# Last pass of a two-layer attention and feed-forward kernel with its gradients: wq read once in full rows, all four groups' products taken in the last head group

## The chip, the cores and the metric

The kernel runs on one core of one Trainium2 chip. The core has TensorE (PE: matmuls and transposes, which write PSUM), VectorE (DVE), ScalarE (ACT), GpSimd (POOL) and SyncE (SP), an on-chip memory SBUF, and 16 DMA engines that move data between SBUF and the chip's main memory. SP issues all loads here and POOL all stores, so there are two DMA queues: SP's (q1 in the profile) and POOL's (q0). Each engine works through its own instruction stream in order.

The metric is the device time of one execution in microseconds. Before the change, the median of three runs is 1944.12 us (1943.76, 1944.12 and 1950.13). About half a per cent, 9.7 us, is what a measurement of this kernel can tell from no change.

## The reference

The forward function is applied to one token `x` (1 x 1024), against a key and a value cache, with the same weights used twice:

```python
def _A_ref(x, k_cache, v_cache, wq, wo):          # 32 query heads, 4 kv heads, 65536 keys, 128 per head
    q = (x @ wq).reshape(B, Sq, Hq, Dh).transpose(0, 2, 1, 3)
    ...
    scores = jnp.einsum("bhqd,bhkd->bhqk", q, k) * (Dh ** -0.5)
    o = jnp.einsum("bhqk,bhkd->bhqd", softmax(scores), v)
    return o.transpose(0, 2, 1, 3).reshape(B, Sq, Hq * Dh) @ wo
def _B_ref(x, w1, b1, w2, b2):                    # 1024 -> 3584 -> 1024, squared relu
    ...
x = x + _A_ref(_layernorm(x), k_cache, v_cache, wq, wo)
x = x + _B_ref(_layernorm(x), w1, b1, w2, b2)
x = x + _A_ref(_layernorm(x), k_cache, v_cache, wq, wo)
x = x + _B_ref(_layernorm(x), w1, b1, w2, b2)
```

The result is that `x` (out_0) and, for a given `grad_out`, the gradients to the input (out_1), the key cache (out_2), the value cache (out_3), wq (out_4), wo (out_5), w1 (out_6), b1 (out_7), w2 (out_8) and b2 (out_9). All inputs and outputs are bfloat16. Each cache is 4 x 65536 x 128, that is 67 MB, and so is its gradient.

## The kernel before, in words

**Four passes over the caches.** The two forward attentions are passes 0 and 1. The backward of the second attention is pass 2, which needs only the gradient to its queries. Pass 3, the last, computes the query gradient of the first attention and the gradients of both caches (which take parts from both attentions), and stores everything that is large. Between the passes stand dense stages for the feed-forward layers. The names in the code are `attn_fwd`, `attn_bwd3` and `attn_bwd4`; the kernel's PSUM flag `PS["pass4"]` is set in the last pass, which begins near 1185 us.

**Items and steps.** A pass goes over four head groups (one per kv head, eight query heads each), and over the 512 columns of 128 keys of each group in items of eight. `pipeline` (L840) runs one step per item: in each step it calls every stage on the item that is due at that stage's lag, and then `bg.step`, which runs one piece of background work. The last pass has 256 items, 64 per group. Its first stage (values, `vT`) leads the others by up to 16 steps and its last (`k8`, L1445, which folds keys into the query gradient) trails by 11 (`B4_LAG`). After the last item of a group `k8` calls `on_group(g)`, here `on4`: from then on the query gradient `dqT` of that group is known.

**Blocks of 1 MB.** SBUF holds an arena of 20 blocks of 1 MB (128 partitions of 8 KB). `Slot` takes a block, `free` gives it back. Eight of the blocks hold the softmax numerators of both attentions, two per group; they come free as the groups of the last pass end. In the last pass blocks are kept in two classes: a ring for blocks that will be stored (`fill=True`), which starts with two blocks, grows to five (`NRING`) and gets two more at the end of each group, and the rest for loads. A load can start when its block's last reader is done.

**Who sets the order.** In passes 0 to 2 the engines' streams keep the order of the program (`manual_schedule`). In the last pass they don't: a planner simulates the program with its own idea of each instruction's duration and, on each engine, puts next the earliest instruction of the program that it takes to be ready. An instruction late in the program can so be moved ahead of others. What the planner expects of a load need not be what the chip does, and on the chip the streams are fixed.

**Background work of the last pass.** `Background.step` (L786) first serves `urgent` generators, one piece per step; a generator that yields `"wait"` lets the `normal` ones have the step. Urgent are:

- `g_dO` (L965), the gradient to the first attention's output for the next group, through `g_rowdots` (L577) over eight slabs of wo;
- `g_dn` (L992), added by `on4` for each of the first three groups: the share of this group's `dqT` in the gradient `dn1` to the layer norm's output, also through `g_rowdots`, over eight slabs of wq.

`g_rowdots` multiplies a slab (128 rows of the weight, 1024 columns) by a vector that `g_bcast_vec` (L559) has spread over all partitions, on VectorE (L598), and sums each row on ScalarE (L587):

```python
        steps = 8 if PS["pass4"] else WAIT_STEPS
        ...
            t = mvs.tile([P, n], BF, name="mv_t", tag="mv_t", bufs=2)
            nc.vector.tensor_tensor(out=t[:, :], in0=slab, in1=vbc[:, :], op=ALU.mult)
```

Slabs come four to a load of 1 MB: for wo, 8 KB that lie together per partition (`wo_runs`, L495); for wq, four pieces of 2 KB per partition, since a group's 1024 columns are a quarter of a row (`wq_slabs`, L487). The second load of a generator is issued when the first block has been used up, and `steps` waits are put ahead of its first product.

Normal are the outer products for the weight gradients (`g_outer`, `g_outer_wide`, `gwq`: two-row matmuls, L1504, whose results go to an arena block through `evac` and from there to memory) and `g_biases`.

**The last group.** Its `dqT` is known only at the very end, so its share is worked out by another way. `pre_load("wq4", ...)` loads its eight slabs in two loads 20 steps before the end, into two blocks. `fill4`, 10 steps before the end, takes two more blocks (`Rows`, L612), turns the slabs on TensorE (`front`, L661, 64 transposes at L682) and copies them, then drains the background. When `on4` is called for the last group, `PRE["rows"].run()` multiplies the turned slabs by `dqT` on TensorE (`back`, L707), and the layer norm's backward, out_1 and the last quarter of out_4 (`g_outer_last`, L1507, stores at L1525) follow.

**Copies out of PSUM.** `evac` (L150) gives each copy to ScalarE or VectorE by a running account of both loads. In `outer16` (L1418) it makes the results of the cache gradients, two copies of 128 x 1024 per step, and every second step a block is stored (L1432).

**The forward output.** `side_x4` (L1849) accumulates the last feed-forward product beside the dense stage between passes 2 and 3, adds it up after that stage's w2 slabs, and calls `col_to_dram` (L202) at once: a transpose on TensorE, a copy on VectorE, a store by POOL.

Of the kernel before, what the change touches and what calls it, by code (L numbers as in the profile page):

```python
# [3 lines left out]

# [12 lines left out]
P = 128  # L17
# [3 lines left out]
def kernel(  # L21
# [128 lines left out]
    def evac(out, in_, kind="bf"):  # L150
# [11 lines left out]
        else:  # L162
            load["dve"] += cd
            nc.vector.tensor_copy(out=out, in_=in_)  # L164


    def col_from_dram(v1d, n, name):
        nj = n // P
# [387 lines left out]
        return t  # L556


    def g_bcast_vec(vcol, nj):  # L559
# [5 lines left out]
        vbc = mvs.tile([P, nj * P], BF, name="vbc", tag="vbc", bufs=1)  # L565
        yield
        for j0 in range(0, nj, 4):
            pg = ps_gg() if PS["pass4"] else ps_tr([P, 512], F32)
            for jj in range(4):
                nc.tensor.matmul(pg[:, jj * P:(jj + 1) * P], lhsT=ident_b[0:nj, j0 + jj:j0 + jj + 1].to_broadcast([nj, P]),  # L570
                                 rhs=rows[0:nj, :], start=True, stop=True)
            nc.scalar.copy(out=vbc[:, j0 * P:(j0 + 4) * P], in_=pg[:, 0:512])
            add_load(act=0.6)
            yield
        return vbc

    def g_rowdots(slab_it, nk, vcol, nj, finish, name):  # L577
        n = nj * P
        y = vec.tile([P, nk], F32, name=name)
        nc.gpsimd.memset(y[:], 0.0)  # L580
        vbc = None
        due = None
        steps = 8 if PS["pass4"] else WAIT_STEPS

        def total(t, kc):
            def f():
                nc.scalar.activation(out=t[:, :], in_=t[:, :], func=ACTF.Copy, accum_out=y[:, kc:kc + 1])  # L587
            return f
        for kc, slab in slab_it:
# [8 lines left out]
            nc.vector.tensor_tensor(out=t[:, :], in0=slab, in1=vbc[:, :], op=ALU.mult)  # L598
# [12 lines left out]

    class Rows:  # L612
        def __init__(self, pool=None, bufs=NWT):
            self.pool, self.bufs = pool, bufs
            self.views = deque()
            self.n = 0
            self.parts = 0
            if pool is None:

                for _ in range(2):  # L620
                    t = Slot("s_wt").t[:, :].rearrange("p (v a b) -> p v a b", v=4, a=8)
# [667 lines left out]
    def attn_bwd4(p, La, Lb, on_group, bg, stack, end=()):  # L1289
# [128 lines left out]
        def outer16(name, out, key, xt, gg, j1):  # L1418

            if j1 == 0:  # L1420
                state[key] = Slot(name, True)
            stg = state[key].t[:, :].rearrange("p (j d) -> p j d", d=DH)
            for m in range(2):
                pg = ps_gg()
                for h in range(2):
                    nc.tensor.matmul(pg[:, 512 * h:512 * h + 512], lhsT=xt[64 * h:64 * h + 64, j1 // 8 + m, :],  # L1426
                                     rhs=gg[64 * h:64 * h + 64, :, :].rearrange("p a b -> p (a b)"),
                                     start=True, stop=True, tile_position=(64 * h, 0))
                jj = j1 + 8 * m
                evac(stg[:, jj:jj + 8, :].rearrange("p j d -> p (j d)"), pg[:, :], kind="f32")  # L1430
            if j1 + 16 == J:
                nc.gpsimd.dma_start(out=out, in_=stg)  # L1432
                state.pop(key).free(stored=True)
# [415 lines left out]
    def side_x4(kc, slab):  # L1849
        for nb in range(DC):  # L1850
            nc.tensor.matmul(ps_x4[:, nb, :], lhsT=d_cols(slab, nb), rhs=L4["gb"][:, kc:kc + 1].to_broadcast([P, 64]),
                             start=kc == 0 and nb == 0, stop=kc == FC - 1 and nb == DC - 1, skip_group_check=True)
        add_load(pe=DC * 0.03)
        if kc == FC - 1:
            f = tmp.tile([P, DC], F32, name="ffn_f")
            nc.vector.tensor_tensor(out=f[:], in0=ps_x4[:, :, 0], in1=b2c[:], op=ALU.add)
            nc.vector.tensor_tensor(out=x4[:], in0=x3[:], in1=f[:], op=ALU.add)
            col_to_dram(x4, D, out_0.rearrange("a b d -> (a b d)"))
    rows.add(w2_slabs()[0], FC, DC, lambda: dx2[:], fin_dh2, mix=True, side=side_x4)
    rows.add(w1_slabs()[0], DC, FC, lambda: dh2[:], fin_dx1, cols=f_cols, mix=True)  # L1860
    rows.add(wo_slabs(firstg[3])[0], R, DC, lambda: dx1[:], dO_finish(L1, firstg[3]), inplace=True)
# [15 lines left out]
    bg.total = 2 + n_outer(FC, DC) + n_outer(DC, FC, True) + n_outer(HQ, DC) + (G - 1) * n_outer(DC, DC)  # L1877
    bg.steps = len(ITEMS[3]) - 4
    dn1 = vec.tile([P, DC], F32, name="dn1")

    def g_biases():
        gb2 = tmp.tile([P, DC], F32, name="gb2")
        nc.vector.tensor_tensor(out=gb2[:], in0=gx[:], in1=dx2[:], op=ALU.add)
        col_to_dram(gb2, D, out_9)
        yield
        gb1 = tmp.tile([P, FC], F32, name="gb1")
        nc.vector.tensor_tensor(out=gb1[:], in0=dh4[:], in1=dh2[:], op=ALU.add)
        col_to_dram_f(gb1, F, out_7)
        yield
# [3 lines left out]
    def gwq(g):  # L1893
        return g_outer(bgpool, out_4, DC, R, [L3["n"], L1["n"]], [L3["dqT"][:, gsl(g)], L1["dqT"][:, gsl(g)]], c0=g * 1024)

    def on4(g):
        if g != lastg[3]:
            bg.add(g_dn(L1, dn1, g, g == firstg[3]))
            bg.normal.append(gwq(g))
        else:  # L1900
            next(PRE["gwq"])
            PRE["rows"].run()
# [22 lines left out]
    ps4_stack.close()  # L1925

# [29 lines left out]
```

## Time and profile before

| What | Value |
|---|---|
| Median of three runs | 1944.12 us |
| The profiled execution's own time | 1939.92 us |
| Its span, from the first to the last instruction | 1938.1 us |
| Moved by DMA in the span | 787.63 MB, 406 GB/s on average |
| Busy share of the span: PE, DVE, ACT, POOL | 82%, 60%, 54%, 7% |
| SP's queue (loads), share of the 16 DMA engines' time | 77.2% |
| POOL's queue (stores) | 20.5% |
| Busy in 1757 to 1922 us (165 us): PE, DVE, ACT | 138.0, 120.3, 116.1 us |

"L598 DVE" is an instruction of line 598 on VectorE. In a table of stretches, each row gives the stretch, its length, the busy time of PE, PE's weight loads, DVE, ACT and POOL with the number of instructions, then TensorE's granted clock as a share of full speed, the mean busy share of the 16 DMA engines (it can read 1.01 where packets overlap a little), and the GB/s that they moved. In a timeline a row gives the start, the duration, the engine, the line, the operation and what it writes and reads; a bracket at the end gives how long the engine sat idle before it and what ended that; "issue" there is a wait that the profile puts down to nothing.

### The profile page before, as it was taken

The page shows a single profiled execution, that of the slowest core. Times are in us where ns is not written, and L with a number is a line of the kernel's source. Part 1 is how long each engine was busy: PE and PEld are TensorE (multiplying, and loading weights), DVE is VectorE, ACT ScalarE, POOL GpSimd, SP SyncE. Part 2 cuts the span into 40 slices and gives each one's busy share as a digit, 9 for nine tenths or more (in the row PEclk, how much of TensorE's full clock was granted, in tenths as well). Part 3 has the DMA queues.
Part 4 walks back from the last instruction along what each step waited for, and adds up shares of the span by engine and source line. Part 5 has one row for each costly group of instructions (what it writes and reads, how often), then busy time and mean ns, then how long its engine had stood idle before and what let it go on. Part 6 is the DMA issues. An engine that isn't in the chain of part 4 may idle for free. (4 is left out here: it accounts for less than half of the span.)

```text
span 1938.1 us, 66986 instructions
## 1 busy us (share of the span) xinstructions
PE 1585.2 (82%) x30199; PEld 1301.4 (67%) x30199; DVE 1170.3 (60%) x2453; ACT 1044.9 (54%) x1617; POOL 142.2 (7%) x321
## 2 busy tenths in 40 slices
PE   6878778688777888977787898889997987697987
PEld 6878777678777877877776886555554654454554
DVE  5655555255555554545454567777775886685876
ACT  3444334245433545445363455766875885575775
POOL 0000000000000000000000001121111211121211
PEclk9999899689999999998899999898997998797998
DMA  9999999999999998999999988999999999899998
GB/s 393 427 425 425 429 427 415 391 407 423 427 425 429 428 422 309 377 425 429 426 424 421 408 314 308 425 424 389 425 424 413 419 424 424 345 419 397 424 422 352
DMA packets 107149, 787.63 MB, mean 406 GB/s; under 512 B 9440, under 2 KB 16622, under 8 KB 42222
## 3 DMA queue, kind: packets, MB, share of 16 engines
q1 hardware_dynamic: 82782, 617.65, 77.2%
q0 software_dynamic: 24080, 165.70, 20.5%
q8 instruction: 236, 3.87, 0.7%
q14 instruction: 51, 0.42, 0.1%
HBM read 617.62 MB, written 165.69 MB: 404 GB/s over the span
## 5 line engine op out<-in xcount | busy, mean ns | idle before, releaser
L164 DVE COPY kt<-ps_tr 128x1024 bf16<-128x1024 bf16 x724 | 496.3, 688 | 429.0 <-PE ps_tr L1024 244.0
L161 ACT CAST arena<-ps_gg 128x1024 bf16<-128x1024 f32 x457 | 444.4, 1011 | 185.0 <-PE ps_gg L1426 137.9
L1024 PE MATMUL ps_tr<-ident_b,arena 128*128 128x128 bf16 x3840 | 308.2, 225 | 36.9 <-DMA arena<-in_A_k_cache_dram 27.5
L161 ACT COPY kt<-ps_tr 128x1024 bf16<-128x1024 bf16 x164 | 171.0, 1046 | 186.1 <-PE ps_tr L1216 103.3
L164 DVE CAST arena<-ps_gg 128x1024 bf16<-128x1024 f32 (+2 forms) x186 | 222.2, 1195 | 77.1 <-PE ps_gg L1426 34.5
L1024 PEld LDWEIGHTS <-arena 128*128 128x128 bf16 x3840 | 232.9, 101 | 44.7 <-DMA arena<-in_A_k_cache_dram 30.3
L1126 PE MATMUL ps_acc<-arena 128*128 128x64 bf16 (+4 forms) x4096 | 205.6, 196 | 60.2 <-DMA arena<-in_A_v_cache_dram 45.1
L1426 PE MATMUL ps_gg<-GG,xt 64*128 64x512 bf16 x1024 | 210.6, 409 | 43.3 <-DVE arena L164 28.3
L1345 PE MATMUL ps_tr<-ident_b,arena 128*128 128x128 bf16 x1824 | 177.4, 232 | 33.7 <-DMA arena<-in_A_v_cache_dram 30.7
L1126 PEld LDWEIGHTS <-arena 128*128 128x128 bf16 x4096 | 159.9, 100 | 66.1 <-DMA arena<-in_A_v_cache_dram 48.7
L1042 PE MATMUL ps_sc<-L_qpad,kt 128*128 128x64 bf16 (+7 forms) x3584 | 183.0, 194 | 16.3 <-issue 8.3
L1107 ACT ACTIVATE arena<-S_sb,L_negm 128x128 bf16<-128x128 f32 x256 | 165.5, 1002 | 55.7 <-DVE L_negm L1092 42.2
L1216 PE MATMUL ps_tr<-ident_b,arena 128*128 128x128 bf16 x1920 | 154.3, 226 | 44.3 <-DMA arena<-in_A_v_cache_dram 43.5
L1345 PEld LDWEIGHTS <-arena 128*128 128x128 bf16 x1824 | 116.8, 103 | 90.7 <-issue 55.2
L1042 PEld LDWEIGHTS <-kt 128*128 128x128 bf16 x3584 | 152.6, 100 | 20.2 <-issue 8.8
L1216 PEld LDWEIGHTS <-arena 128*128 128x128 bf16 x1920 | 117.1, 101 | 48.8 <-DMA arena<-in_A_v_cache_dram 46.1
L1457 PEld LDWEIGHTS <-arena 128*128 128x128 bf16 x2048 | 92.2, 101 | 57.8 <-issue 39.9
L1107 ACT ACTIVATION_READ_ACCUMULATOR arena<-S_sb,L_negm 128x1 f32 x256 | 127.9, 500 | 0.0
L1426 PEld LDWEIGHTS <-xt 64*128 64x128 bf16 x1024 | 64.5, 94 | 90.1 <-issue 52.3
L587 ACT ACTIVATE mv_t<-mv_t 128x1024 bf16<-128x1024 bf16 x96 | 102.1, 1065 | 35.8 <-DVE mv_t L598 35.8
L1382 PE MATMUL ps_sc<-DOB,kt 128*128 128x64 bf16 (+3 forms) x1824 | 112.3, 197 | 0.1
L1270 PE MATMUL ps_acc<-dsT,arena 128*128 128x64 bf16 (+7 forms) x2048 | 103.1, 194 | 11.3 <-DMA arena<-in_A_k_cache_dram 7.8
(317 smaller groups left out, 2154.0 us busy)
## 6 DMA issues: line engine op xcount, KB each, us to landing
arena<-in_A_k_cache_dram SPq DMA_DIRECT2D x82, 2048.0 KB, 21.7
arena<-in_A_v_cache_dram SPq DMA_DIRECT2D x79, 2048.0 KB, 21.7
out_dram<-arena POOLq DMA_DIRECT2D x149, 1024.0 KB, 16.2
arena<-in_A_v_cache_dram SPq DMA_DIRECT2D x84, 1024.0 KB, 14.2
arena<-in_A_k_cache_dram SPq DMA_DIRECT2D x84, 1024.0 KB, 14.6
arena<-in_A_wo_dram SPq DMA_DIRECT2D x22, 1024.0 KB, 19.6
arena<-in_B_w_dram SPq DMA_DIRECT2D x21, 1024.0 KB, 9.2
arena<-in_A_wq_dram SPq DMA_DIRECT2D x18, 1024.0 KB, 18.0
```

What stands on the lines that cost most here:

```text
L161: nc.scalar.copy(out=out, in_=in_)
L164: nc.vector.tensor_copy(out=out, in_=in_)
L587: nc.scalar.activation(out=t[:, :], in_=t[:, :], func=ACTF.Copy, accum_out=y[:, kc:kc + 1])
L1024: nc.tensor.transpose(pt[:, i, :], kb8[:, i, :], ident_b[:, :])
L1042: nc.tensor.matmul(state["ps_s"][:, s:s + w, :].rearrange("p a b -> p (a b)"), lhsT=kt[:, i, :], rhs=L["qpad"][:, g, 0:w, :].rearrange("p ...
L1107: nc.scalar.activation(out=E(p, g, c0, SU)[:, :, h], in_=S[:, h, :], func=ACTF.Exp, bias=L["negm"][:, g, su, h:h + 1], scale=SCALE, accum_ ...
L1126: nc.tensor.matmul(ps_o[:, 0:w, :], lhsT=vb8[:, i, :], rhs=E(p, g, c, w), start=(c % SU == 0), stop=(c % SU == SU - 1), skip_group_check=True)
L1216: nc.tensor.transpose(pt[:, i, :], vb8[:, i, :], ident_b[:, :])
L1270: nc.tensor.matmul(ps_dq[:, 0:w, :].rearrange("p a b -> p (a b)"), lhsT=kb8[:, i, :], rhs=dsT[:, s:s + w, :].rearrange("p a b -> p (a b)") ...
L1345: nc.tensor.transpose(pt[:, i, :], vb8[:, i, :], ident_b[:, :])
L1382: nc.tensor.matmul(state["ps_dp"][:, s:s + w, :].rearrange("p a b -> p (a b)"), lhsT=vt[:, i, :], rhs=DOB[:, g, 0:w, :].rearrange("p a b - ...
L1426: nc.tensor.matmul(pg[:, 512 * h:512 * h + 512], lhsT=xt[64 * h:64 * h + 64, j1 // 8 + m, :], rhs=gg[64 * h:64 * h + 64, :, :].rearrange(" ...
```

## The change

Five edits:

- **All `dn` products in the last group.** `on4` no longer adds `g_dn` for each of the first three groups. When the third group ends, it adds one generator, `g_dn_rows`, for all three. It spreads three vectors (24 columns) into one arena block, and then goes over wq in eight loads of 1 MB, each 128 full rows of 4096 columns, 8 KB per partition. Per load: three waits, then the last group's part of the rows is turned on TensorE (`front`), then the three other groups' parts are multiplied and summed on VectorE and ScalarE. The two blocks for turned slabs and the block for the vectors come from the ring, as soon as the third group ends. The preload `wq4` is gone, and `fill4` only drains.
- **Places.** `mark_place` notes the last matmul and the last copy of each `outer16` result in the program. `in_place` binds what is traced under it behind the noted instruction of the same engine, so that the planner can't put it further ahead. It is used for the slab products of `g_rowdots` and `g_dn_rows` on VectorE, and for the transposes of `front` on TensorE.
- **Waits.** `steps` in `g_rowdots` is 3 in place of 8 in the last pass; with 3, no wait follows the spreading of the vector (there were four).
- **out_0.** `col_to_dram(x4, ...)` moves from `side_x4` to the start of `g_biases`, in the last pass.
- The count `bg.total`, by which the normal work is spread over the steps, has 3 in place of 2 for the pieces of `g_biases`.

```diff
+    def mark_place():
+        i = nc.cur_bb.bb.instructions[-1]
+        PIN[i.engine] = i
+    @contextmanager
+    def in_place(engine):
+        if engine not in PIN:
+            yield
+        else:
+            with tc.issue_after(PIN[engine]):
+                yield
...
-        steps = 8 if PS["pass4"] else WAIT_STEPS
+        steps = 3 if PS["pass4"] else WAIT_STEPS
...
-            nc.vector.tensor_tensor(out=t[:, :], in0=slab, in1=vbc[:, :], op=ALU.mult)
+            with in_place(mybir.EngineType.DVE):
+                nc.vector.tensor_tensor(out=t[:, :], in0=slab, in1=vbc[:, :], op=ALU.mult)
...
+                mark_place()
                 evac(stg[:, jj:jj + 8, :].rearrange("p j d -> p (j d)"), pg[:, :], kind="f32")
+                mark_place()
...
-            col_to_dram(x4, D, out_0.rearrange("a b d -> (a b d)"))
...
     def g_biases():
+        col_to_dram(x4, D, out_0.rearrange("a b d -> (a b d)"))
+        yield
...
+    def g_dn_rows(gs):
+        n = R * P
+        v = rows_of(A_wq)
+        vsl = Slot("s_vbc", True)
+        y = vec.tile([P, DC, len(gs)], F32, name="dn1_y")
+        nc.gpsimd.memset(y[:, :, :], 0.0)
+        PRE["rows"] = Rows(ring=True)
+        job = PRE["rows"].job(DC, R, lambda: L1["dqT"][:, gsl(lastg[3])], dn_finish(dn1, False))
+        for k, g in enumerate(gs):
+            yield from g_bcast_vec(L1["dqT"][:, gsl(g)], R, vsl.t[:, k * n:(k + 1) * n])
+        def product(sl, kc, k):
+            t = mvs.tile([P, n], BF, name="mv_t", tag="mv_t", bufs=2)
+            with in_place(mybir.EngineType.DVE):
+                nc.vector.tensor_tensor(out=t[:, :], in0=sl.t[:, gs[k] * n:(gs[k] + 1) * n], in1=vsl.t[:, k * n:(k + 1) * n], op=ALU.mult)
+            nc.scalar.activation(out=t[:, :], in_=t[:, :], func=ACTF.Copy, accum_out=y[:, kc, k:k + 1])
+            add_load(dve=0.1 + n * 0.00054, act=0.42 + n * 0.00083)
+        for kc in range(DC):
+            sl = Slot("s_wqr")
+            nc.sync.dma_start(out=sl.t[:, :], in_=v[:, kc, :])
+            for _ in range(3):
+                yield "wait"
+            NOW["slab"] = sl
+            with in_place(mybir.EngineType.PE):
+                run(PRE["rows"].front(job, kc, sl.t[:, lastg[3] * n:(lastg[3] + 1) * n]))
+            product(sl, kc, 0)
+            yield
+            for k in range(1, len(gs)):
+                product(sl, kc, k)
+            sl.free()
+            yield
+        vsl.free()
+        nc.vector.tensor_reduce(out=dn1[:], in_=y[:, :, :], axis=AX.X, op=ALU.add)
...
     def on4(g):
         if g != lastg[3]:
-            bg.add(g_dn(L1, dn1, g, g == firstg[3]))
             bg.normal.append(gwq(g))
+            if L1["dn_of"][-1] == g:
+                bg.add(g_dn_rows(L1["dn_of"]))
...
     def fill4():
-        PRE["rows"] = Rows()
-        PRE["rows"].add(PRE["wq4"], DC, R, lambda: L1["dqT"][:, gsl(lastg[3])], dn_finish(dn1, False))
-        PRE["rows"].fill()
         bg.drain()
...
-    attn_bwd4(3, L1, L3, on4, bg, b4, [(12 + B4_LAG, last_v), (20, pre_load("wq4", lambda: wq_slabs(lastg[3], 2))), (10, fill4)])
+    attn_bwd4(3, L1, L3, on4, bg, b4, [(12 + B4_LAG, last_v), (10, fill4)])
```

More of the change, by code (lines that the diff above doesn't have):

```diff
@@ L1 @@
-from contextlib import ExitStack
+from contextlib import ExitStack, contextmanager
 from collections import deque
@@ L164, in evac @@
             nc.vector.tensor_copy(out=out, in_=in_)
+    PIN = {}
+    def mark_place():
[8 more added lines that the diff above has]
+                yield
     def col_from_dram(v1d, n, name):
@@ L556, in to_cols_bf, with g_bcast_vec @@
         return t
-    def g_bcast_vec(vcol, nj):
+    def g_bcast_vec(vcol, nj, vbc=None):
         pt = ps_mv([nj, P], F32)
@@ L564, in g_bcast_vec @@
         nc.vector.tensor_copy(out=rows[0:nj, :], in_=pt[:, :])
-        vbc = mvs.tile([P, nj * P], BF, name="vbc", tag="vbc", bufs=1)
+        if vbc is None:
+            vbc = mvs.tile([P, nj * P], BF, name="vbc", tag="vbc", bufs=1)
         yield
@@ L612, with __init__ @@
     class Rows:
-        def __init__(self, pool=None, bufs=NWT):
+        def __init__(self, pool=None, bufs=NWT, ring=False):
             self.pool, self.bufs = pool, bufs
@@ L620, in __init__ @@
                 for _ in range(2):
-                    t = Slot("s_wt").t[:, :].rearrange("p (v a b) -> p v a b", v=4, a=8)
+                    t = Slot("s_wt", ring).t[:, :].rearrange("p (v a b) -> p v a b", v=4, a=8)
                     self.views.extend(t[:, v, :, :] for v in range(4))
@@ L1876 @@
     bg.normal.append(g_outer_wide(bgpool, out_6, DC, FC, [L4["n"], L2["n"]], [dh4, dh2]))
-    bg.total = 2 + n_outer(FC, DC) + n_outer(DC, FC, True) + n_outer(HQ, DC) + (G - 1) * n_outer(DC, DC)
+    bg.total = 3 + n_outer(FC, DC) + n_outer(DC, FC, True) + n_outer(HQ, DC) + (G - 1) * n_outer(DC, DC)
     bg.steps = len(ITEMS[3]) - 4
@@ L1894, in gwq @@
         return g_outer(bgpool, out_4, DC, R, [L3["n"], L1["n"]], [L3["dqT"][:, gsl(g)], L1["dqT"][:, gsl(g)]], c0=g * 1024)
+    L1["dn_of"] = [g for g in dict.fromkeys(g for g, _ in ITEMS[3]) if g != lastg[3]]
+    def g_dn_rows(gs):
[30 more added lines that the diff above has]
+        nc.vector.tensor_reduce(out=dn1[:], in_=y[:, :, :], axis=AX.X, op=ALU.add)
+        yield
     def on4(g):
         if g != lastg[3]:
-            bg.add(g_dn(L1, dn1, g, g == firstg[3]))
             bg.normal.append(gwq(g))
+            if L1["dn_of"][-1] == g:
+                bg.add(g_dn_rows(L1["dn_of"]))
         else:
```

## The prediction

> **What bounds the kernel now.** I read the stretches of the last pass first, then who waited for whom, then the timelines around the stretches that stand out. Stretches (columns as told above: length, five busy times, granted clock, DMA share, GB/s):
>
> ```profile
> 1340.00:1490.00 150.00, 128.86 (x1572) 81.09 (x1571) 109.51 (x196) 110.87 (x134) 26.76 (x53) 0.89 1.01 424
> 1490.00:1505.00 15.00, 12.91 (x157) 8.68 (x158) 10.80 (x16) 9.64 (x13) 2.15 (x4) 0.77 0.96 388
> 1505.00:1665.00 160.00, 138.20 (x1853) 88.53 (x1851) 121.84 (x229) 118.44 (x142) 28.83 (x55) 0.94 1.01 422
> 1665.00:1695.00 30.00, 17.43 (x213) 11.21 (x212) 16.71 (x28) 14.64 (x20) 3.24 (x7) 0.72 0.77 301
> ...
> 1775.00:1785.00 10.00, 4.72 (x47) 3.21 (x46) 5.61 (x10) 4.51 (x6) 1.07 (x2) 0.57 0.89 339
> ...
> 1900.00:1925.00 25.00, 23.27 (x362) 15.83 (x362) 20.41 (x41) 19.02 (x22) 4.15 (x7) 1.00 0.99 392
> ```
>
> The full stream of transfers (share 1.01, 424 GB/s) bounds the pass; no engine does. Time is lost only where the share falls. An engine's idle time inside a full stream costs nothing: between 1620 and 1630 us TensorE worked for 1.4 us, and the share was 1.01.
>
> Three of the dips follow a wait of VectorE for a slab of wq. The waits of 1560 to 1938 us (total, times, longest), then VectorE's timeline:
>
> ```profile
> DVE mv_t L598 <- issue: 27.8, 3, 14.0
> ```
> ```profile
> 1660.72 0.42 DVE L164 COPY xt<-ps_tr 128x512 bf16<-128x512 bf16 x1
> 1675.15 0.69 DVE L598 TENSOR_TENSOR mv_t<-arena,vbc 128x1024 bf16<-128x1024 bf16 x1 [14.02 <-issue]
> ```
>
> VectorE stands for 14.02 us at a product whose load SP had issued at 1655.77. TensorE then waits 12.17 us for a PSUM copy, no block comes free, SP has nothing to issue, and the stream runs dry at 1672. The other waits at L598 are 5.45 us (to 1485.50), 3.66 (to 1577.66; a slab of wo) and 10.08 (to 1778.34).
>
> Why so early? In the compiled stream of this kernel the product at 1675 is traced at step 177 (its load at 169) and stands among instructions of step 165: the planner moved it ahead by 12 steps of 2.8 us ((1922-1200)/256). And the load is slow. Time to landing of the eight loads of wq, then of the six of wo, both 1 MB:
>
> ```profile
> DMA to landing us min/median/max: 18.0/22.6/27.3
> ```
> ```profile
> DMA to landing us min/median/max: 9.2/9.9/10.6
> ```
>
> The queues' rows of 1767 to 1774 us, while the last such load ran, show why (packets, MB, share):
>
> ```profile
> q0 software_dynamic: 312, 2.28, 77.5%
> q1 hardware_dynamic: 324, 0.64, 23.7%
> ```
>
> Both queues got as many packets through, but the load's are 2 KB and the stores' 8 KB. While wo was loaded (1372 to 1382 us) the two queues moved 2.14 and 2.11 MB.
>
> One more stall concerns the change. In the dense stage TensorE, which is the busy engine there (10.00 us of 1150 to 1160), stands for out_0's transpose:
>
> ```profile
> 1147.22 0.27 PE L205 MATMUL ps_mv<-ident_f,x 128*8 128x128 f32 x1 [2.15 <-DVE x L1857]
> ```
>
> **The change part by part**, against the profiled execution's own 1939.92 us (its span of 1938.1 and 1.8 around it), which lies 4.2 under the median, 1944.12.
>
> *Products leave groups two and three.* The dips at 1490 and 1665 go with them. By share they cost (1.01-0.96) x 15 = 0.75 us and (1.01-0.77) x 30 = 7.2; by GB/s (424-388)/424 x 15 = 1.3 and (424-301)/424 x 30 = 8.7. The dip at 1775 (1.2 by share, 2.0 by rate) lies in the last group, where slabs remain. I take 7.95: the first two, by share, since the slow packets behind a dip may have another cause. Ends: nothing, where the stream breaks elsewhere, and 12.0, all three by rate. What is late next is a load for TensorE inside a full stream, as at 1620.
>
> *Full rows.* wq's 8.39 MB of the last pass are 4096 packets of 2 KB, 84.4 ns each on average by the trace's packet records, on 16 engines: 21.6 us. The 8 KB packets of the same stretch take 314.3 ns: 1024 of them are 20.1 us. Saved 1.5; ends 0 and 1.7 (medians, 84 and 309 ns). The Trainium skill, DMA: Bandwidth & Descriptors, section Specifications, puts line rate at 512 bytes and more, by which 2 KB and 8 KB would run alike and this term would be nothing (the sum 10.95). The packets disagree (388 against 417 GB/s), so the measurement decides.
>
> *out_0.* 2.15 us of standing leave TensorE in the dense stage, where the chain to dh2 (1151.55) runs through it. I take 2.0; ends 0 and 2.3 (with part of the transpose itself). In the last pass the transpose, a copy of 0.28 and POOL's issue of 0.68 (POOL is busy for 18% there) lie beside a full stream: 0. A wait on TensorE there is far below the 3.66 us that caused no dip.
>
> *Later work in the last group.* The first two groups' products move there: 16 of 0.68 us on VectorE (10.9), 16 sums of 1.07 + 0.20 on ScalarE (20.3), two more spreadings (four casts of 0.59, 2.3). Also 4.2 MB of loads move: 9.9 us at 424 GB/s, which the earlier groups lose. The last group took 165 us (1757 to 1922) with 120.3 us of VectorE and 116.1 of ScalarE; it would have 131 and 139 in 175. Cost 0, under the cover of the stream; without the cover, 22.6.
>
> *Waits and places.* A load of full rows has 3 steps, 8.5 us, in program order, and SP is ahead of the program (the slab traced at 169 was issued when VectorE stood near 165). I expect it to land as wo's do, in 9.9 us. Behind a waiting product stand VectorE's copies, for which TensorE waits; behind a waiting transpose, the value blocks' transposes. The trace prices such a stall: 3.66 us made no dip, 5.45 cost 0.75, 10.08 cost 1.2, 14.02 cost 7.2. For g_dO the first product of the second load is traced 9 steps earlier, at 73 in place of 82 for the third group; it already stands among 75 to 78. 0; end 3 x 0.75 = 2.3 lost.
>
> *Queues and blocks.* SP issues eight loads of wq (0.38 us each) as before, now all among the last group's k and v loads, eight waits for a block in place of four. The ring gives up three blocks; it has five in the first group and two more per group ended, so 11 - 3 = 8 in the last. In the first group, with five, the dip of 1310 to 1340 (368 GB/s) cost (424-368)/424 x 30 = 4.0 us. Eight is nearer to the later groups: 0; end 4.0 lost. The load class no longer gives up four blocks near the end.
>
> *The end.* The 64 transposes of 1907 to 1915 (0.55 us per eight, 4.4) and eight copies of 0.69 move earlier. In 1900 to 1925 the stream lost (424-392)/424 x 25 = 1.9. Counting the background's steps, four pieces of normal work are left for the drain in place of two, two copies of 1.2. I take 1.0 gained; ends 1.9 gained and 2.4 lost.
>
> The sum: 7.95 + 1.5 + 2.0 + 1.0 = 12.45 us, 1927.5 for an execution like the profiled, and 1944.12 - 12.45 = 1931.7 as a median. With all upper ends, 17.9: 1926.2, or 1922.0 on the profiled execution.
>
> **Rivals.**
>
> *The dip moves.* Only out_0 and the packets pay: 1944.12 - 3.5 = 1940.6; with the ring's 4.0 and the drain's 2.4 lost, 1947. For it: the dip at 1310 has no product in it, and the planner orders the whole pass anew. Against: three of four dips have the one cause.
>
> *Slabs late in the last group (slower).* If a slab's product lands in the stream one step ahead of its place (the noted copy on VectorE may be a step old, since most go to ScalarE) and the load still takes wq's shortest 18.0 us, VectorE stands 18.0 - 2 x 2.82 = 12.4 us; between 10.08 and 14.02 the price is 4.7, eight times 37.6: 1944.12 + 37.6 - 12.45 = 1969. It passes the gain from 10.3 us per slab (1.56 x 8 = 12.5) and half a per cent more than before from 11.1 (2.77 x 8 = 22.2). At wo's 9.9 us the stall is 4.3 and costs under 0.75. Against: the packets.
>
> *The last group bound by ScalarE (slower).* 1944.12 - 12.45 + 22.6 = 1954.3. Against: 139 us in 175.
>
> **How the numbers follow.** Forecast 0.62, the dip moves 0.22, late slabs 0.11, ScalarE 0.05. A difference of over 0.5% (9.7 us, what a measurement of this kernel can tell from none) is below 1934.4. Of the forecast's 0.62, some 0.53 lie below it and 0.09 above; of the moved dip's, 0.02 below, 0.20 within. Late slabs and ScalarE give 0.14 slower, 0.02 within. Faster 0.55, same 0.31, slower 0.14. The range is 1922 to 1946: the forecast with its ends (its own range is 1922 to 1938) and the moved dip without its worst.
>
> **What would show it.** Right: no wait over 6 us at the products' line on VectorE; no dip below 0.95 between 1340 and 1700; wq's landing near 10 us; queue rows with 2 KB packets gone from the last pass; no stall at out_0's transpose; transposes of turned slabs spread over the last group. Wrong: a dip of over 5 us in the first three groups without a product in it, eight waits of over 10 us on VectorE or TensorE in the last group, or ScalarE above 95% there.

## The result, and the profile after

The changed kernel takes 1962.40 us (median of six runs, 1960.05 to 1965.42), the kernel before 1943.95 beside it: 1.0089 of the time before, 95% interval 1.0072 to 1.0106. It is slower by 0.89%, some 17 us by this ratio, and 30.7 us behind the forecast of 1931.7. The profiled execution took 1962.58 us (span 1960.7), against 1939.92 (span 1938.1).

In the third group the forecast came true. The stretches of the changed kernel at the times at which the kernel before had its dips (length, five busy times, granted clock, DMA share, GB/s):

```profile
1490.00:1505.00 15.00, 13.03 (x155) 8.11 (x152) 8.80 (x20) 9.87 (x11) 2.21 (x4) 0.84 1.01 425
1505.00:1665.00 160.00, 142.24 (x1884) 89.90 (x1883) 121.06 (x220) 117.13 (x136) 30.66 (x57) 0.93 1.01 424
1665.00:1695.00 30.00, 25.48 (x272) 15.16 (x270) 16.83 (x27) 18.24 (x20) 4.87 (x10) 0.77 1.01 424
1775.00:1785.00 10.00, 9.59 (x131) 6.36 (x131) 8.12 (x11) 7.19 (x8) 2.41 (x4) 1.00 1.01 424
1900.00:1925.00 25.00, 23.05 (x327) 15.42 (x327) 21.53 (x40) 18.93 (x26) 3.38 (x6) 0.89 0.77 294
```

The row of 1665 to 1695 has a share of 1.01 where it had 0.77. The last row is the news: 0.77 where there was 0.99. In the second group the dip at 1490 went too, but there is a new one. The stretch before the change, the same after it, and the wait of TensorE for a value block that ends in it:

```profile
1410.00:1420.00 10.00, 9.64 (x92) 5.70 (x93) 6.58 (x9) 5.89 (x9) 1.15 (x2) 0.66 1.02 428
```
```profile
1410.00:1420.00 10.00, 8.38 (x84) 4.86 (x85) 4.33 (x6) 5.32 (x6) 0.53 (x1) 0.63 0.75 317
```
```profile
1411.48 0.40 PE L1363 MATMUL ps_tr<-ident_b,arena 128*128 128x128 bf16 x2 [11.96 <-DMA arena<-in_A_v_cache_dram]
```

The waits of VectorE between 1560 and 1938 us, and the products' line (L1934) in them:

```profile
DVE kt L164 <- PE ps_tr L1363: 31.9, 36, 3.9
...
DVE mv_t L1934 <- ACT mv_t L1935: 0.9, 2, 0.5
```

No product waits for its load. The eight loads of full rows, and the transfers of the whole run:

```profile
DMA to landing us min/median/max: 8.1/12.7/15.1
```
```profile
DMA packets 104077, 787.63 MB, mean 402 GB/s; under 512 B 9440, under 2 KB 16622, under 8 KB 38126
```

They land in 12.7 us (22.6 before), and 4096 packets of 2 KB have become 1024 of 8 KB (107149 packets before, 42222 of them under 8 KB). So where is the time? The groups of the last pass end when `dqT` is written. The last group and what lies behind it (the tail, from here on), of the kernel before, then of the changed one:

```profile
1741.70:1919.80 178.10, 147.52 (x1958) 94.18 (x1957) 125.28 (x224) 121.37 (x140) 31.17 (x56) 0.90 1.00 412
1919.80:1938.10 18.30, 8.25 (x97) 3.79 (x93) 8.01 (x19) 7.08 (x7) 4.52 (x7) 0.70 0.66 269
```
```profile
1742.00:1931.80 189.80, 144.98 (x1891) 95.64 (x1887) 126.28 (x212) 120.91 (x155) 28.33 (x50) 0.82 0.90 361
1931.80:1960.70 28.90, 15.65 (x136) 6.29 (x131) 14.54 (x31) 14.47 (x17) 5.77 (x9) 0.63 0.62 255
```

The third group ends at the same time in both (1741.7, 1742.0). The last one then takes 11.7 us longer, and the tail 10.6. VectorE and ScalarE are about as busy in the last group as before (126.3 us against 125.3, and 120.9 against 121.4), so more work of theirs is not the likely reason. The share of the transfers falls to 0.90.

How far each execution is ahead of (-) or behind (+) the kernel before's, in us, at the moment when so many MB have been moved (from the start times of the trace's packets; runs of the next section are listed too):

| MB moved | changed | nowork | pins | pins_bound | k_bound | after_bound_early |
|---|---|---|---|---|---|---|
| 490 | +0.7 | -1.2 | +1.3 | +4.4 | +2.9 | +0.1 |
| 600 | +6.0 | +1.9 | +8.2 | +5.8 | +5.7 | +1.9 |
| 650 | +4.0 | +0.9 | +6.1 | +3.7 | +4.6 | +1.7 |
| 690 | -5.1 | -8.2 | +4.9 | +4.8 | -4.5 | -7.3 |
| 750 | -1.4 | -8.9 | +3.6 | +4.8 | -5.4 | -8.8 |
| 770 | +8.2 | -9.0 | +3.6 | +4.9 | -5.6 | -9.2 |
| 787 | +22.8 | -4.3 | +7.9 | +8.1 | +4.6 | -2.3 |

The changed kernel loses 5.3 us between 490 and 600 MB, gains 9.1 between 650 and 690 MB and loses 27.9 from there to the end.

A k load is a load of a block of the key cache, and the dq products are the matmuls of the stage `k8` that use it (L1457 before, L1477 after). TensorE's waits for k loads in the last group, before and after; then the timelines of TensorE and of SP around one such wait, and the wait of SP that ends in it:

```profile
PE ps_acc L1457 <- DMA arena<-in_A_k_cache_dram: 11.2, 2, 10.7
```
```profile
PE ps_acc L1477 <- DMA arena<-in_A_k_cache_dram: 29.1, 7, 10.2
```
```profile
1815.26 0.23 PE L1400 MATMUL ps_sc<-DOB,kt 128*128 128x64 bf16 x2
1825.70 0.66 PE L1477 MATMUL ps_acc<-X,arena 128*128 128x64 bf16 x9 [10.21 <-DMA arena<-in_A_k_cache_dram]
1826.29 0.60 PE L1509 MATMUL ps_gg<-ident_b,r_cc 128*2 128x128 bf16 x8
1826.82 1.03 PE L1363 MATMUL ps_tr<-ident_b,arena 128*128 128x128 bf16 x8
```
```profile
1809.10 0.33 SPq L381 DMA_DIRECT2D arena<-in_A_k_cache_dram  x1
1809.52 0.44 SPq L381 DMA_DIRECT2D arena<-in_A_v_cache_dram  x1
1827.88 0.33 SPq L1939 DMA_DIRECT2D arena<-in_A_wq_dram  x1
```
```profile
SPq L1939 <- PE ps_tr L1363: 22.3, 2, 17.8
```

This is a circle, in which one wait prepares the next. TensorE stands at a dq product (L1477) for a k load issued at 1809.10. Behind it in TensorE's order stand the transposes of a value block (L1363), which give that block back. SP needs it for its next slab, issues nothing from 1809.52 to 1827.88, and the loads behind the slab are late too: the next k load goes out at 1835.37, and TensorE waits 5.29 us for it, to 1846.48. Between 1826 and 1834 us the stream's share is 0.83, and between 1844 and 1854 it is 0.30. The kernel before waits for k loads for 11.2 us in its last group, the changed one for 29.1.

### The profile page after: what moved, and what is told of

Read it like the earlier page. It is cut to its first block, busy times and chain, and to the rows that moved or that the text cites. A ratio compares the mean times of both kernels' runs of the same rounds, so it can differ in the third digit from the quotient of the medians.

```text
span 1960.7 us, 67021 instructions
## 1 busy us (share of the span) xinstructions
PE 1597.4 (81%) x30199; PEld 1308.3 (67%) x30199; DVE 1170.4 (60%) x2448; ACT 1045.7 (53%) x1620; POOL 144.1 (7%) x319
## 4 chain that ended last, share of the span: by engine, by line
DMA 48%; PE 33%; ACT 7%; DVE 6%; issue 5%; SPq 0%; POOL 0%; POOLq 0%; ACTq 0%; DVEq 0%
DMA arena<-in_A_v_cache_dram 20%; DMA arena<-in_A_k_cache_dram 19%; DMA out_dram<-arena 8%; PE ps_tr L1042 5%; ACT arena L161 4%; PE ps_gg L1444 4%; PE ps_tr L1363 3%; PE ps_acc L1144 3%; PE ps_sc L1060 3%; PE ps_tr L1234 2%; DMA arena<-in_B_w_dram 2%; DVE arena L164 2%; PE ps_sc L1400 1%; PE ps_acc L1477 1%; PE ps_sc L1260 1%
## 5 line engine op out<-in xcount | busy, mean ns | idle before, releaser
L161 ACT CAST arena<-ps_gg 128x1024 bf16<-128x1024 f32 x454 | 443.0, 1010 | 215.4 <-PE ps_gg L1444 125.3
L1444 PE MATMUL ps_gg<-GG,xt 64*128 64x512 bf16 x1024 | 211.7, 418 | 37.1 <-ACT arena L161 18.0
L1363 PE MATMUL ps_tr<-ident_b,arena 128*128 128x128 bf16 x1824 | 174.9, 233 | 21.3 <-DMA arena<-in_A_v_cache_dram 19.7
L1363 PEld LDWEIGHTS <-arena 128*128 128x128 bf16 x1824 | 118.4, 104 | 73.5 <-issue 49.5
L1477 PEld LDWEIGHTS <-arena 128*128 128x128 bf16 x2048 | 89.6, 102 | 84.4 <-DMA arena<-in_A_k_cache_dram 47.4
L1477 PE MATMUL ps_acc<-X,arena 128*128 128x64 bf16 (+3 forms) x1536 | 91.3, 199 | 34.8 <-DMA arena<-in_A_k_cache_dram 34.8
L1444 PEld LDWEIGHTS <-xt 64*128 64x128 bf16 x1024 | 61.2, 94 | 85.0 <-issue 49.0
## 6 DMA issues: line engine op xcount, KB each, us to landing
arena<-in_A_k_cache_dram SPq DMA_DIRECT2D x84, 1024.0 KB, 12.4
```

The source lines that it names most:

```text
L161: nc.scalar.copy(out=out, in_=in_)
L1363: nc.tensor.transpose(pt[:, i, :], vb8[:, i, :], ident_b[:, :])
L1477: nc.tensor.matmul(ps_dq[:, 0:w, :].rearrange("p a b -> p (a b)"), lhsT=kb8[:, i, :], rhs=X[:, s:s + w, :].rearrange("p a b -> p (a b)"), ...
```

## The experiments

Six theories were on the table. W: the work moved into the last group. B: too few blocks for loads or stores there. H: a slab's block held until its last product. P: the places (`in_place`). T: ordinary background work left for the tail. And, formed from the first eight runs, O: the order on TensorE.

**Places and waits (pins).** `mark_place`, `in_place` on the product of `g_rowdots`, `steps = 3`; nothing else of the change.

> The kernel before with only the second part of the change: the places in the order (mark_place, in_place on the product of g_rowdots) and three waiting steps in place of eight. Each group still reads its own quarter of wq, out_0 stays in the dense stage, no three blocks leave the ring. If the products that waited for their loads were what the prediction took them for, the waits of 14.02 and 10.08 us at the products' line go and the time is 1944 - 8 = about 1936. If the dips have another cause (the blocks, the stores), it stays within 4 us of 1944. If the places themselves do harm, it is above 1950, and the loss of the changed kernel is theirs.

1949.23 us, 1.0033 of before (1.0021 to 1.0045), which lies between two of the cases expected. No product waits any more, but the gain does not come. TensorE's timeline:

```profile
1622.65 0.66 PE L1476 MATMUL ps_acc<-X,arena 128*128 128x64 bf16 x9 [14.12 <-DMA arena<-in_A_k_cache_dram]
```

With the products' stall gone, a wait for a k load stands in its place.

**Without the products (nowork).**

```
     def product(sl, kc, k):
-        t = mvs.tile(...)
-        ... tensor_tensor ... activation(accum_out=y[:, kc, k:k + 1]) ... add_load
+        pass
```

> The changed kernel with the 24 products of g_dn_rows and their 24 sums left out (out_1 is therefore not the reference's); the full rows are still read, held for as long and turned for the last group. Theory W (more work on VectorE and ScalarE in the last group, some 16 us and 26 us): back to 1944 or below. Theory B (blocks: a slab holds one of seven load blocks all through the last group and three blocks are taken out of the ring, so that loads are issued late): little changes, 1955 to 1962.

1935.69 us, 0.9961 (0.9945 to 0.9976). The last group:

```profile
1738.90:1909.40 170.50, 144.21 (x1911) 93.43 (x1908) 110.86 (x189) 107.28 (x118) 29.00 (x51) 0.87 1.00 413
```

The same loads in the same blocks cost nothing when the products are gone. That speaks against B, and for W, H or P.

**Blocks (ring_to_load2, before_less1, slab_in_ring).** In turn: two free blocks are taken out of `RING` when `g_dn_rows` starts; in the kernel before, a `Slot` is held from the third group's end to `fill4`; `sl = Slot("s_wqr", True)`.

> The changed kernel, but two blocks go from the ring to the loads when the full rows begin: nine blocks for loads, nine in the ring, three of which are taken, so six are left for stores. Theory B with the loads as the short side: waits of SP for a block fall, TensorE's waits for k loads in the last group (10.21, 5.29, 8.32 us) go, 1962 comes down by 5 to 15 us. If the ring is the short side: stores wait, and it is slower than 1962. Theory W: no change (1960 to 1965).

> The kernel before with one of its seven load blocks held idle from the end of the third group to ten steps before the end of the pass: one cause that theory B names, alone, without any more work or bytes in the last group. Theory B: dips and waits for k loads appear in the last group, 1944 becomes 1950 to 1960. Theory W or a theory of the tail: 1944, within 3 us.

> The changed kernel with the slabs of full rows in blocks of the ring, so that all seven load blocks stay with the k and v loads; the ring, which has given three, gives one more. Theory B/H (the loads of k and v lose one block of seven to slabs): TensorE's waits for k loads in the last group shrink from 35 us to under 15 us, 1945 to 1953. If the ring is as short: stores are awaited on ScalarE and VectorE and it stays above 1958.

ring_to_load2: 1961.03 us, 1.0091 (1.0072 to 1.0109), no change. slab_in_ring: 1957.66, 1.0070 (1.0050 to 1.0090); TensorE still waits 29.4 us for k loads between 1742 and 1925 (29.1 in the changed kernel, not the 35 of the expectation). Here SP waits 102.7 us for stores to give back ring blocks, so this run is no clean test of B. before_less1: 1952.73, 1.0048 (1.0035 to 1.0061). The last groups, of ring_to_load2, slab_in_ring and before_less1:

```profile
1737.90:1925.40 187.50, 139.15 (x1877) 92.37 (x1875) 127.72 (x213) 121.19 (x155) 27.27 (x48) 0.85 0.91 372
```
```profile
1739.20:1926.30 187.10, 140.26 (x1889) 92.92 (x1887) 127.40 (x212) 120.89 (x155) 28.43 (x50) 0.86 0.92 367
```
```profile
1743.40:1933.80 190.40, 152.72 (x1959) 95.94 (x1957) 126.31 (x224) 122.02 (x140) 31.16 (x56) 0.86 0.95 389
```

A block less does hurt, as B says, by 9.4 us in the kernel before. But two blocks more do not heal the changed one. B is a way to lose time, and ring_to_load2 speaks against its being the way here.

**Holding and places (off_slab, no_places).**

```
-  in0=sl.t[:, gs[k] * n:(gs[k] + 1) * n]      # off_slab
+  in0=vsl.t[:, k * n:(k + 1) * n]
...
-        if engine not in PIN:                  # no_places
+        if True:
             yield
```

> The changed kernel, with the 24 products of g_dn_rows at their places but reading only the spread vectors, not the slab (out_1 is therefore not the reference's). VectorE and ScalarE do the same work; only the slab's block is given back by the transposes, as in the run without products, and no longer by the last product. Theory H (it is the holding of the block, up to the last product of a later step): as without products, 1936 to 1945, last group near 171 us at a DMA share of 1.00. Theory W (the engines' work): stays at 1955 to 1965.

> The changed kernel with in_place doing nothing: products and turning transposes are ordered by their estimated times like everything else. Theory P (a product that is bound behind a copy of its step stands late, and with it the slab's block): 1940 to 1952. Theory H and W: about 1962; and a product that is ordered ahead of its load waits for it, as at the 14.02 us of the kernel before, so 1962 to 1975.

off_slab: 1961.40 us, 1.0092 (1.0077 to 1.0107). no_places: 1946.39, 1.0016 (1.0000 to 1.0033). H falls. So does W: with all the work, but without places, 14 us come back by the ratios (16 by the medians). The last group of no_places, and its products' waits there:

```profile
1742.90:1920.30 177.40, 145.78 (x1913) 95.69 (x1911) 128.98 (x220) 125.63 (x160) 28.70 (x51) 0.87 0.98 397
```
```profile
DVE mv_t L1934 <- DMA arena<-in_A_wq_dram: 17.3, 4, 6.6
DVE mv_t L1934 <- issue: 5.6, 1, 5.6
```

Products now wait 22.9 us for their loads, which the places were there to prevent (one of the waits, 5.6 us, is put down to nothing by the profile), and yet the group is 12.4 us shorter than in the changed kernel.

**The order.** What does a place on VectorE do to TensorE? The compiled order tells. For each transpose of a value block in the last group one counts how many steps the newest dq product ahead of it on TensorE is in advance of the transpose's own step; the mean of this is the lead. (The run called tail is told below.)

| kernel | lead, steps | last group, us | kernel | lead, steps | last group, us |
|---|---|---|---|---|---|
| nowork | 0.1 | 170.5 | tail | 2.0 | 193.6 |
| no_places | 0.1 | 177.4 | off_slab | 2.9 | 186.4 |
| before | 0.3 | 178.1 | changed | 3.2 | 189.8 |
| k_bound | 0.0 | 174.1 | ring_to_load2 | 4.1 | 187.5 |
| | | | slab_in_ring | 4.2 | 187.1 |

(before_less1 has 0.3 and 190.4: there a block was missing.) The order in which the traces record the two kinds of matmul ranks the nine kernels of this table in the same way. With the products' places the planner orders the dq products up to eight steps early, so that TensorE asks for a k load before the value block that has to make room. nowork, without the products of `g_dn_rows` but with all other places, has a lead of 0.1, and so has no_places: the lead comes with the places of these products. Why the planner does so was not looked into. The size of the lead does not rank the loss: tail has the smallest of the five in the right half and the longest last group. That this order on TensorE makes the loss is theory O, and one edit tests it: the first dq product of a step is queued behind the newest value block's last transpose, in the last group only.

```
             vb8[:, i, :], ident_b[:, :])
+                VT["last"] = nc.cur_bb.bb.instructions[-1]
...
+  with (tc.issue_after(VT["last"]) if i == 0 and "last" in VT and g == items[-1][0] else ExitStack()):
       nc.tensor.matmul(ps_dq[:, 0:w, :] ...)
```

> Theory O (order): in the compiled order of the changed kernel the dq products of a step (L1477, which need a k load) stand 3.2 steps on average, at most 8, ahead of the transposes of the same step's value block (L1363) in the last group, against 0.3 in the kernel before, 0.1 in the runs without products and without places, 2.9 with the products off the slab and 4.2 with the slabs in the ring. TensorE so asks for a k load early and holds up the transposes that would give SP its next block. Here one thing is changed in the changed kernel: in the last group the first dq product of a step is queued on TensorE behind the transposes traced last before it (ahead by 0.0). All places, products and blocks are as in the changed kernel. Theory O: TensorE's waits for k loads in the last group fall from 29 us to under 12 us, dqT comes 170 to 180 us after the third group's, and 1962 becomes 1942 to 1952. If the lead is only a companion of the loss: 1957 to 1965.

1940.98 us, 0.9998 (0.9979 to 1.0017): the whole loss is gone, with the code of places, products and blocks untouched. Its last group and tail, and TensorE's waits for k loads in the group:

```profile
1742.50:1916.60 174.10, 142.49 (x1899) 93.20 (x1897) 129.18 (x218) 122.97 (x159) 29.05 (x51) 0.87 0.97 402
1916.60:1942.60 26.00, 14.02 (x123) 6.09 (x121) 12.52 (x26) 11.52 (x13) 5.22 (x8) 0.60 0.56 229
```
```profile
PE ps_acc L1481 <- DMA arena<-in_A_k_cache_dram: 9.8, 1, 9.8
```

Waits of 29.1 us have become one of 9.8. In the chain of work that ended last, k loads are 40.1% of the changed kernel's last group and 10.8% of this one's. O is shown for the last group, with one reserve: this edge, too, lets the planner order the last group anew.

**The tail (tail).** `Background.step` returns after a step of urgent work; here ordinary work of the same step goes on while `g_dn_rows` runs.

> The changed kernel, where a step of g_dn_rows no longer keeps the ordinary background work of the same step from running. What is left behind the last dqT (28.9 us against 18.3 before) is the suspect: theory T says that the loss of the tail comes from ordinary work that 28 steps of the full rows pushed back; then the tail is 19 to 23 us and 1962 becomes 1953 to 1957. Otherwise the tail stays at 27 to 30 us (cache gradients that the late stream itself leaves), and the time with it.

1956.23 us, 1.0065 (1.0039 to 1.0092). The tail, against 28.90 us:

```profile
1933.50:1954.40 20.90, 8.13 (x99) 3.83 (x96) 10.26 (x20) 7.22 (x8) 4.50 (x7) 0.74 0.50 203
```

What is gone from it is read from the groups of instructions in the tail, of the kernel before, the changed one and this one:

```profile
L161 ACT CAST arena<-ps_gg 128x1024 bf16<-128x1024 f32 x7 | 7.1, 1012 | 4.9 <-PE ps_gg L1504 4.0 <-PE ps_gg L1426 1.0
L164 DVE CAST arena<-ps_gg 128x1024 bf16<-128x1024 f32 x4 | 4.9, 1220 | 0.7 <-PE ps_gg L1504 0.7
```
```profile
L161 ACT CAST arena<-ps_gg 128x1024 bf16<-128x1024 f32 x13 | 13.1, 1011 | 6.8 <-PE ps_gg L1524 4.5 <-PE ps_gg L1444 2.2
L164 DVE CAST arena<-ps_gg 128x1024 bf16<-128x1024 f32 x8 | 9.8, 1223 | 5.4 <-PE ps_gg L1524 4.0 <-PE ps_gg L1444 1.4
```
```profile
L164 DVE CAST arena<-ps_gg 128x1024 bf16<-128x1024 f32 x7 | 8.6, 1223 | 1.9 <-PE ps_gg L1445 0.9 <-PE ps_gg L1525 0.7 <-DMA out_dram<-arena 0.3
L161 ACT CAST arena<-ps_gg 128x1024 bf16<-128x1024 f32 x6 | 6.1, 1012 | 4.5 <-PE ps_gg L1525 3.0 <-PE ps_gg L1445 1.5
```

21 casts of gradients lie behind the last `dqT` in the changed kernel, 11 before, 13 here. T is right for the tail, by 8.0 us. But the last group is 3.8 us longer than in the changed kernel, and the gain in time, 1.0065 against 1.0089, is not clear of noise.

**Both, and the first three groups (before_bound, after_bound_tail, noplaces_bound_tail).** The binding through the whole pass: in the kernel before; in the tail's kernel; in the tail's kernel without places.

> The kernel before with the same binding through the whole last pass, and nothing else. There the dq products stand 3.0 steps ahead in the first group, 0.8, 0.5 and 0.3 in the others. Theory O: a few us in the first group and the waits of 10.7 us for loads: 1934 to 1944. If a lead of this size is harmless, or the binding costs TensorE time: 1944 to 1955.

> The changed kernel with the binding through the whole pass and with ordinary background work let through in the steps of the full rows. If both causes are right and independent (about 12 us in the last group, 8 to 10 us behind the last dqT), 1962 becomes 1935 to 1945. If what one frees the other takes, 1946 to 1956.

> The same, and the places of the products and turning transposes left out. If the places cost only through the lead of the dq products, this equals the run with places within 4 us. If they help where the lead is gone (products that do not wait for a load), it is 4 to 15 us slower than that one; if they harm otherwise too, it is faster, 1928 to 1938.

1948.12 us, 1.0024 (1.0011 to 1.0037); 1940.14, 0.9983 (0.9967 to 0.9998); 1943.01, 1.0001 (0.9986 to 1.0015). Binding alone is no gain, so the lead of 3.0 steps that the kernel before has in its first group cost nothing that can be seen: a lead need not cost time. The runs with and without places lie 2.9 us apart, within the 4 us expected if places cost only through the lead; that they help where it is gone is not clear of noise.

**Whose is the gain (pins_bound, pins_bound_x4).** Places and binding in the kernel before, without and with the move of out_0.

> The kernel before with the places and three waiting steps for the products (no full rows, out_0 stays) and the dq products bound behind the value blocks through the whole pass. Places alone gave 1.0033 of before, binding alone 1.0024. If the predicted gain of the first three groups is real and needs both (no product that waits, no load asked for early), it is ahead by 8 to 13 us at 690 MB, and as its last group and tail are those of the kernel before, it ends at 1930 to 1936. If the gain came with the full rows, 1941 to 1950.

> The same with out_0's store moved to the last pass. By the prediction's term 2.0 us less than the run without (ends 0 to 2.3); if the stall of 2.15 us at out_0's transpose had other work beside it, within 1 us of it.

1947.36 us, 1.0011 (0.9999 to 1.0023), and 1948.09, 1.0020 (1.0006 to 1.0033). So the gain at 650 to 690 MB came with the full rows, and of a gain by out_0's move nothing is seen. In pins_bound no product waits and no dq product runs ahead, yet the dip is there:

```profile
1645.00:1675.00 30.00, 21.59 (x303) 14.36 (x303) 19.51 (x41) 18.01 (x25) 3.35 (x6) 0.81 0.79 309
```

It costs (1.01-0.79) x 30 = 6.6 us, against the 7.2 that were put down to a waiting product. In the table above every kernel that loads no wq in the third group gains 9.0 to 9.1 us at this place; the two that do load it, with no product waiting, gain 1.2 and lose 1.1. What in these loads makes the dip was not tested; in pins_bound TensorE waits 6.60 us for a k load there and 3.39 for a value block.

**The end (after_bound_early, k_bound_tail).** after_bound_tail with `bg.steps = len(ITEMS[3]) - 16` in place of - 4; and k_bound with the tail's edit.

> The changed kernel with binding through the whole pass, background work let through in the steps of the full rows, and all ordinary background work due twelve steps earlier. If the end is late for that work, 1940 becomes 1932 to 1937 and the stretch behind the last dqT stays at or under 21 us; if the full rows' own loads end the last group late, it stays at 1938 to 1943.

> The changed kernel with the binding in the last group alone and background work let through in the steps of the full rows. k_bound was 1941 with 26.0 us behind the last dqT; if only the tail goes to some 21 us, 1936; against the run bound through the whole pass (1940) it shows what the binding does in the first three groups: by the stream at 690 MB (13.1 us against 4.5 us ahead) this one should be up to 8 us slower, 1940 to 1948, if that lead lasts to the end.

1938.15 us, 0.9968 (0.9956 to 0.9981), the fastest that computes everything, though by 0.3% only; and 1943.58, 0.9994 (0.9982 to 1.0006), no gain over k_bound, although its tail is 21.8 us: its last group is 178.9. With the order put right, work taken out of the tail so returned nothing. The last group and the tail of after_bound_early:

```profile
1741.90:1913.60 171.70, 140.36 (x1924) 92.62 (x1923) 130.82 (x221) 125.39 (x160) 27.98 (x50) 0.92 1.00 420
1913.60:1935.60 22.00, 11.17 (x95) 5.41 (x91) 7.59 (x19) 6.65 (x7) 3.96 (x6) 0.50 0.41 168
```

The last group now runs at a full share with all the work in it. Of its 9.2 us ahead at 770 MB 6.9 are lost again by 787 MB: the tail moves 168 GB/s, where the kernel before moved 269. The gain of the first three groups is largely given back there; whether the background's work or the full rows' loads make that end late is left open. after_bound_tail and k_bound_tail differ by the binding in the first three groups; their 3.4 us are not clear of noise.

## Why the prediction was wrong

- *Waits and places* ("0; end 3 x 0.75 = 2.3 lost") is the step that failed. It asked who stands behind a waiting product or transpose, and so priced places by waits alone, from a list of waits and the dips behind them; of that list the largest, 14.02 us for 7.2, falls as well, since pins_bound has the dip without the wait. No product waited. But an edge in one engine's order changes the planner's order on the others: the dq products went 3.2 steps ahead of the value blocks, and TensorE's own waits for k loads rose from 11.2 to 29.1 us. Undoing that order returns some 18 us by the ratios (1.0089 to 0.9998; 21.4 us by the medians, 1962.40 and 1940.98).
- *The end* ("1.0 gained; ends 1.9 gained and 2.4 lost") failed too. The tail grew by 10.6 us. Of the ten casts more in it, of 1.0 and 1.2 us, each with two matmuls ahead of it, four belong to outer products of the background (24 matmuls of L1524 against 16 of L1504) and five to cache gradients (16 of L1444 against 6 of L1426). The term counted two more pieces of background and no cache gradients. k_bound still has a tail of 26.0 us, 7.7 over the kernel before, and lies 9.3 us above the forecast.
- *Products leave groups two and three* (7.95): 9.1 us where the large dip was, so the size was right, but the reason was not: the dip goes with wq's loads, not with the waiting product, and that the size fits is luck. In the second group 5.3 us had been lost before, about where TensorE waits 11.96 us for a value block at 1411 us; at the third group's end (710 MB) 5.7 us are left.
- *Full rows* (1.5): no run isolates it. The loads land in 12.7 us, not in the 9.9 expected; that was soon enough for the products.
- *out_0* (2.0): the stall left TensorE, and nothing came of it (pins_bound_x4 beside pins_bound). At 490 MB the changed kernel is 0.7 us late. No gain is seen, but each of the two runs is known only to some 2.5 us, so a term of 2.0 can't be told from 0 well.
- *Later work in the last group* (0) was right: k_bound has all of it and a last group of 174.1 us, shorter than before. (By the writing of `dqT` the last group of the kernel before took 178.1 us, 1741.7 to 1919.8, not the 165 from 1757 to 1922; the cover is only larger for it.) *Queues and blocks* (0) was right as well, by k_bound and ring_to_load2, though a block is worth 9.4 us in the kernel before.
- None of the rivals was it. The slabs were not late, ScalarE was busy for 120.9 of 189.8 us, and 1962 lies above the range because the longer last group (11.7 us) and the longer tail (10.6) came together.

## What to carry to other kernels

Where a planner orders the engines' work, price an ordering edge by what the planner does to the other engines, and compare the compiled orders before the waits: a wait that is taken away on one engine can come back on another. On an engine that works strictly in order, look for circles, in which the work that frees a buffer stands behind work that waits for a load, so that the next loads come late for want of that buffer. And a stall at the head of a dip need not be its cause; only a run that removes the stall and keeps the rest can tell.

## What the runs showed of the hardware

With full rows the queue of the loads got nearly as many bytes through as that of the stores. The queues' rows of 1768 to 1782 us of the changed kernel, while the second such load ran beside loads of k and v (packets, MB, share):

```profile
q0 software_dynamic: 436, 3.15, 53.5%
q1 hardware_dynamic: 375, 2.79, 47.5%
```

The two queues move 3.15 and 2.79 MB, where with 2 KB pieces it was 2.28 and 0.64 from 312 and 324 packets. The Trainium skill, DMA: Bandwidth & Descriptors, section Queues, rings and completion order, says that an engine goes round its queues packet by packet. The near packet counts of both pairs of rows fit that, if the page's packet, which can hold several descriptors, is the one that the profile counts; no run here shows whether it is. In these rows the size of a load's pieces, not only their number, goes with its queue's share of a contended stream; the median landing time of the loads of wq fell from 22.6 to 12.7 us.
